# Filler matmuls on TensorE at the end of a cached-attention decode kernel

## The chip, the cores and the metric

The kernel runs on one core of a Trainium2 chip. The metric is the device time of one execution in microseconds (us), the median of several runs. Profiles are single executions; their span is about 1.9 us shorter than the device time of the same run.

## The reference

Two branches on one token are mixed by a sigmoid gate. Branch A is grouped-query attention with 32 query heads over a cache of 4 key/value heads and 65,536 positions; branch B is a small gated MLP.

```python
def reference(A_x, A_k_cache, A_v_cache, A_wq, A_wo, B_x, B_w_in, ..., gate_w):
    x = A_x                                     # 1 x 1 x 1024, bf16
    g = sigmoid((x * gate_w).sum(-1))
    q = (x @ A_wq)                              # 32 heads of 128
    p = softmax(q @ K^T * 128 ** -0.5)          # K cache: 4 x 65536 x 128, 64 MB
    a = (p @ V) @ A_wo                          # V cache as large; A_wo 4096 x 1024, 8 MB
    b = gelu_mlp(x, B_w_in, ..., B_w_out)
    return g * a + (1 - g) * b
```

All of K, V and the weights are read once, about 162 MB, for one output row of 1024 numbers. (The sizes of single tensors and tiles are in units of 2^20 bytes; the 162 MB is in units of 10^6.)

## The kernel before

One queue streams everything into five tiles of 4 MB that are reused; w_in comes in one piece of 7 MB, which is so in both kernels.

```python
    win = load(win_view, (KC, F), 3)
    win_t = [win[:, i * KH:(i + 1) * KH, :] for i in range(2)]
    ...
    def v_tile(g, j, vt):                # 32 matmuls of 512 columns, 64 output rows each
    ...
    def head_out(g):                     # last normalization of a head group, mostly VectorE
        nc.vector.tensor_tensor(out=om8, in0=o_ps[g]..., in1=own_8..., op=ALU.mult)
        nc.vector.tensor_reduce(out=o_sb[:], in_=om8.rearrange("p x d -> p d x"), ...)
        nc.tensor.matmul(om_ps[gs, DH:], lhsT=hs, rhs=lss[g][:], ...)
        nc.tensor.matmul(om_ps[gs, :DH], lhsT=hs, rhs=o_sb[:], ...)
        ...                              # five short VectorE steps that end in oa
    def project(w, n, vec, c0, first=False, last=False):
        for c in range(n):               # n rows of wo per partition
            for t in range(NB):          # 4 matmuls side by side, 32 output rows each
                nc.tensor.matmul(out_ps[t * B:(t + 1) * B, :],
                    lhsT=vec[:, c0 + c:c0 + c + 1].to_broadcast([P, B]),
                    rhs=w[:, c, t * NO:(t + 1) * NO], ...)
```

The end of the program, which the change touches (WO_SPLIT gives pieces of 16, 8, 4, 2, 1 and 1 rows):

```python
    for j, n, at in ((0, 2, 1), (2, 1, 3), (3, 1, 4)):
        for i, vt in enumerate(load_kv(A_v_cache, G - 1, j, at, n)):
            v_tile(G - 1, j + i, vt)
    head_out(G - 1)
    c0 = 0
    for at, split in enumerate(WO_SPLIT):
        for n in split:
            t = load(wo_view[:, c0:c0 + n, :], (n, D), ...)
            project(t, n, oa, c0, last=(c0 + n == OC))
            c0 += n
    nc.scalar.copy(out=out_sb[:], in_=out_ps[:])
    ...                                  # two stores of the row
```

Of the kernel before, what the change touches and what calls it, by code (L numbers as in the profile page):

```python
# [8 lines left out]
FP32 = mybir.dt.float32  # L9
# [6 lines left out]
P = 128  # L16
# [6 lines left out]
ZN = 448  # L23
HN = 512
WO_SPLIT = ((16,), (8, 4, 2, 1, 1))


@with_exitstack
def kernel(
# [15 lines left out]
    nc = tc.nc  # L45

    _, _, D = A_x.shape
    _, G, S, DH = A_k_cache.shape
# [15 lines left out]
    assert S % (P * CT) == 0 and F == 2 * NB * ZN and ZN == B * FC and HD == NHB * NB * HN  # L64
    assert NHB * NB == 2 * G and CC * B == 2 * HN and sum(map(sum, WO_SPLIT)) == OC

# [5 lines left out]
    pss = ctx.enter_context(tc.tile_pool(name="pss", bufs=2, space=bass.MemoryType.PSUM))  # L72
# [6 lines left out]
    def same_weights(ins):  # L79
        held.add(ins.ins.name)  # L80
# [79 lines left out]
    def load(src, shape, at):  # L160
        n = 1
        for s in shape:
            n *= s
        v = kv[:, int(at * CT * P):int(at * CT * P) + n]
        if len(shape) == 2:
            v = v.rearrange("p (a b) -> p a b", b=shape[1])
        ins = nc.sync.dma_start(out=v, in_=src)  # L167
        if not first_load:
            first_load.append(ins.ins.name)
        return v  # L170

    def load_kv(src, g, j, at, n=1):
        h, i = divmod(j, 2)
        rows = src[0, g, 2 * h * CT * P:2 * (h + 1) * CT * P, :].rearrange(
            "(p c) d -> p (c d)", c=2 * CT)
        v = load(rows[:, i * CT * DH:(i + n) * CT * DH], (n * CT * DH,), at)
        return [v[:, i * CT * DH:(i + 1) * CT * DH] for i in range(n)]
# [27 lines left out]
    wt = [big.tile([P, VC, BP, NB, VC, REP], BF16, name=f"wt{i}") for i in range(2)]  # L205
# [15 lines left out]
    def one_hot(shape, dtype, in0, col, name):  # L221
# [13 lines left out]
                     start=True, stop=True)  # L235
# [107 lines left out]
    for k in range(NHB):  # L343
# [15 lines left out]
                     rhs=q4[:].rearrange("p t x -> p (t x)"), start=True, stop=True)  # L359
# [71 lines left out]
    def v_tile(g, j, vt):  # L431
        if j == 0:
            o_ps[g] = pso.tile([P, 2, VC * DH], FP32, name="o_ps")
        vx = vt.rearrange("p (v c d) -> p c v d", v=VC, d=DH)
        for u in range(CC // 2):
            hs = slice(u % 2 * P // 2, (u % 2 + 1) * P // 2)
            for e in range(2):
                ins = nc.tensor.matmul(  # L438
                    o_ps[g][hs, e, :],
                    lhsT=ptt[g, j][:, 2 * u:2 * u + 2, :].rearrange("p c x -> p (c x)"),  # L440
                    rhs=vx[:, 2 * u + e], start=(j == 0 and u < 2),
                    stop=(j == NT - 1 and u >= CC // 2 - 2), skip_group_check=True)
                if e > 0:
                    same_weights(ins)

    def head_out(g):
        gs = slice(g * B, (g + 1) * B)
        nc.vector.tensor_tensor(  # L448
            out=om8, in0=o_ps[g][:].rearrange("p e (v d) -> p (e v) d", d=DH),
            in1=own_8[:].unsqueeze(2).to_broadcast([P, 2 * VC, DH]), op=ALU.mult)  # L450
        o_sb = wk.tile([P, DH], FP32, name="o_sb")
        nc.vector.tensor_reduce(out=o_sb[:], in_=om8.rearrange("p x d -> p d x"), axis=AX.X,  # L452
                                op=ALU.add)
        om_ps = psm.tile([P, DH + NT], FP32, name="om_ps", tag="m")
        hs = hsel[:].rearrange("p h q -> p (h q)")
        nc.tensor.matmul(om_ps[gs, DH:], lhsT=hs, rhs=lss[g][:], start=True, stop=True,
                         skip_group_check=True)
        nc.tensor.matmul(om_ps[gs, :DH], lhsT=hs, rhs=o_sb[:], start=True, stop=True,  # L458
                         skip_group_check=True)
        rl = wk.tile([P, 2], FP32, name="rl")  # L460
        nc.vector.reduce_sum(out=rl[gs, 0:1], in_=om_ps[gs, DH:], axis=AX.X)
        nc.vector.reciprocal(out=rl[gs, 1:2], in_=rl[gs, 0:1])
        om = wk.tile([P, QD, OC], FP32, name="om")
        nc.vector.tensor_tensor(
            out=om[gs], in0=om_ps[gs, :DH].rearrange("p (q c) -> p q c", c=OC),
            in1=own_q[gs, :].unsqueeze(2).to_broadcast([B, QD, OC]), op=ALU.mult)
        osum = wk.tile([P, OC], FP32, name="osum")
        nc.vector.tensor_reduce(out=osum[gs, :], in_=om[gs].rearrange("p q c -> p c q"),  # L468
                                axis=AX.X, op=ALU.add)
        nc.vector.tensor_scalar(out=oa[gs, :], in0=osum[gs, :], scalar1=rl[gs, 1:2],  # L470
                                scalar2=gate[gs, :], op0=ALU.mult, op1=ALU.mult)

    NO = D // NB
    out_ps = psl.tile([P, NO], FP32, name="out_ps")

    def project(w, n, vec, c0, first=False, last=False):
        for c in range(n):
            for t in range(NB):
                nc.tensor.matmul(  # L479
                    out_ps[t * B:(t + 1) * B, :],  # L480
                    lhsT=vec[:, c0 + c:c0 + c + 1].to_broadcast([P, B]),
                    rhs=w[:, c, t * NO:(t + 1) * NO],
                    start=(first and c == 0), stop=(last and c == n - 1),
                    skip_group_check=True)
# [22 lines left out]
    for j, n, at in ((0, 2, 1), (2, 1, 3), (3, 1, 4)):  # L507
        for i, vt in enumerate(load_kv(A_v_cache, G - 1, j, at, n)):
            v_tile(G - 1, j + i, vt)
    head_out(G - 1)  # L510


    wo_view = A_wo.rearrange("(p c) n -> p c n", c=OC)
    c0 = 0
    for at, split in enumerate(WO_SPLIT):
        for n in split:
            t = load(wo_view[:, c0:c0 + n, :], (n, D), at + c0 % (OC // 2) * D / (CT * P))
            project(t, n, oa, c0, last=(c0 + n == OC))
            c0 += n
    out_sb = const.tile([P, NO], BF16, name="out_sb")  # L520
    out_rows = out.rearrange("o t (q n) -> (o t q) n", n=NO)
    nc.scalar.copy(out=out_sb[:], in_=out_ps[:])  # L522
    for i, queue in enumerate((nc.scalar, nc.sync)):
        p0 = (2 * i + 1) * B - 1
        ins = queue.dma_start(out=out_rows[2 * i:2 * i + 2, :], in_=out_sb[p0:p0 + 2, :])
# [40 lines left out]
```

## Time and profile before

| | before |
|---|---|
| device time, first three runs | 383.21 us (383.08 to 383.30) |
| span of the profile | 381.3 us |
| bytes from HBM, mean rate | 162 MB, 425 GB/s |
| TensorE / VectorE busy | 60% / 57% |
| last piece of wo landed | 378.81 us |

The page of the profile cuts the span into 40 slices. Its rows give the granted TensorE clock and the busy share of the DMA engines in tenths.

```profile
span 381.3 us, 2579 instructions
...
PE 230.5 (60%) x1372; PEld 56.4 (15%) x796; DVE 218.4 (57%) x211; ACT 39.6 (10%) x55; POOL 4.4 (1%) x10
...
PEclk9995659998859995989589958895989579969766
DMA  9999999999999999999999999999999999999995
```

The DMA engines are at 9 tenths or more in every slice but the last: the kernel is bound by memory traffic. The Trainium skill, "DMA: Bandwidth & Descriptors", section "Where 436 GB/s comes from", puts the ceiling of the fabric at 435 GB/s; the mean here, 425 GB/s, lies just below it.

The chain of waits of before, its last pieces in order of time (start, length, what), without the pieces called issue, 0.04 us at most:

```profile
347.03 31.79 DMA kv<-in_A_wo_dram
378.86 0.43 PE out_ps L479 x4
379.31 0.37 ACT out_sb L522
```

The last wo load ends at 378.81 us. Only the four matmuls of the last row, ScalarE's copy and the store come after it. Of these, TensorE's clock can touch the 0.43 us alone.

The timeline of TensorE at the end of before (start, length, engine, line, operation, shape, count; in brackets the idle time before, and what ended it):

```profile
368.37 0.64 PE L458 MATMUL om_ps<-o_sb,hsel 128*32 128x128 f32 x2 [3.07 <-DVE o_sb L452]
370.39 4.64 PE L479 MATMUL out_ps<-kv,oa 128*32 128x256 bf16 x96 [1.39 <-DVE oa L470]
376.28 0.62 PE L479 MATMUL out_ps<-kv,oa 128*32 128x256 bf16 x16 [1.25 <-DMA kv<-in_A_wo_dram]
377.54 1.06 PE L479 MATMUL out_ps<-kv,oa 128*32 128x256 bf16 x12 [0.64 <-DMA kv<-in_A_wo_dram]
378.86 0.41 PE L479 MATMUL out_ps<-kv,oa 128*32 128x256 bf16 x4 [0.25 <-DMA kv<-in_A_wo_dram]
```

From 376.28 on, each group starts when its data land. TensorE is idle before each of them, so it is not late.

The same stretch of before, cut into windows of 3.41 us whose edges are those of the granted clock. The columns are the window, its length, then busy us (and records) of PE, PEld, DVE, ACT and POOL, then the granted clock, the DMA share and GB/s:

```profile
363.95:367.36 3.41, 1.35 (x14) 0.34 (x6) 2.14 (x2) 0.00 (x0) 0.00 (x0) 1.00 0.93 399
367.36:370.77 3.41, 1.02 (x10) 0.48 (x14) 2.14 (x6) 0.00 (x0) 0.00 (x0) 0.50 0.99 423
370.77:374.19 3.42, 3.42 (x72) 2.59 (x64) 0.00 (x0) 0.00 (x0) 0.00 (x0) 0.50 0.95 392
374.19:377.60 3.41, 1.52 (x52) 1.10 (x44) 0.00 (x0) 0.00 (x0) 0.00 (x0) 1.00 0.85 329
377.60:381.01 3.41, 1.35 (x16) 0.43 (x15) 0.00 (x0) 0.37 (x1) 0.00 (x0) 0.50 0.05 19
```

The clock is either full or half, and it changes only at these edges: a window that is busy enough is followed by one at full clock, a slack one by one at half. The last row, after 377.60, meets the half clock. Two windows of before from the middle of the kernel, each with its successor, bear on how much is enough for full-width matmuls of 512 columns: seven kept the clock, six lost it. (The DMA columns count a packet whole in the window in which it starts, so a short window can show more than 1.00 and more than the mean rate.)

```profile
200.11:203.52 3.41, 1.37 (x7) 0.29 (x3) 3.41 (x2) 0.00 (x0) 0.00 (x0) 1.00 0.93 404
203.52:206.94 3.42, 2.82 (x13) 0.57 (x6) 3.42 (x5) 0.00 (x0) 0.00 (x0) 1.00 1.20 517
237.65:241.07 3.42, 1.18 (x6) 0.28 (x3) 3.42 (x2) 0.00 (x0) 0.00 (x0) 1.00 1.20 517
241.07:244.48 3.41, 3.41 (x10) 0.60 (x5) 3.16 (x2) 0.00 (x0) 0.00 (x0) 0.50 0.89 384
```

In the profile of after:

```profile
200.26:203.67 3.41, 1.30 (x7) 0.29 (x3) 3.41 (x2) 0.00 (x0) 0.00 (x0) 1.00 0.85 365
203.67:207.09 3.42, 3.42 (x10) 0.58 (x4) 3.42 (x5) 0.00 (x0) 0.00 (x0) 0.50 1.20 517
```

### The profile page before, as it was taken

To read this page: it belongs to the slowest core of one execution; us is meant where nothing else is said; L and a number is where in the kernel's file an instruction comes from. 1 tells how busy PE (TensorE), PEld (TensorE's weight loads), DVE (VectorE), ACT (ScalarE), POOL (GpSimd) and SP (SyncE) were. 2 spreads that over 40 slices of the span, in tenths; PEclk is the share of its full clock that TensorE was granted. 3 is DMA by queue.
4 is the path that set the end of the run, shared out by engine and by line. 5 is a ranking of instruction groups with operands and counts; after the bars stand their busy time and mean duration, and the time that the engine had idled before them with its cause. 6 is when DMAs were issued, how large, how long until landed. Compare 5 with 4: busy or idle time off the path is not lost.

```text
span 381.3 us, 2579 instructions
## 1 busy us (share of the span) xinstructions
PE 230.5 (60%) x1372; PEld 56.4 (15%) x796; DVE 218.4 (57%) x211; ACT 39.6 (10%) x55; POOL 4.4 (1%) x10
## 2 busy tenths in 40 slices
PE   0064467678157934796397638872976196849355
PEld 0011011112011200121011101120111011212123
DVE  4133487996687506966977059669960488560040
ACT  1001001111601100114011001040100010500000
POOL 4000000000000000000000000000000000000000
PEclk9995659998859995989589958895989579969766
DMA  9999999999999999999999999999999999999995
GB/s 385 440 433 416 423 429 440 440 485 429 407 412 419 440 442 433 433 433 440 440 428 440 440 440 440 435 434 399 419 440 435 426 440 427 426 414 433 437 412 225
DMA packets 4231, 162.17 MB, mean 425 GB/s; under 512 B 504, under 2 KB 508, under 8 KB 892
## 3 DMA queue, kind: packets, MB, share of 16 engines
q1 hardware_dynamic: 4180, 162.01, 98.7%
q8 instruction: 8, 0.13, 0.1%
q14 instruction: 3, 0.02, 0.0%
q10 hardware_dynamic: 40, 0.01, 0.0%
HBM read 162.01 MB, written 0.00 MB: 425 GB/s over the span
## 4 chain that ended last, share of the span: by engine, by line
DMA 57%; PE 24%; DVE 14%; ACT 2%; issue 1%; SPq 1%; DVEq 0%; ACTq 0%
DMA kv<-in_A_k_cache_dram 42%; PE s_ps L392 20%; DMA kv<-in_A_wo_dram 8%; DVE kv L385 8%; DMA kv<-in_A_v_cache_dram 7%; PE o_ps L438 3%; DVE pt L428 2%; DVE o_sb L452 1%; DVE mx L387 1%; ACT sc L403 1%; ACT sc L425 1%; SPq L167 1%; DVE rowt L448 1%; PE om_ps L458 0%; DVE osum L468 0%
## 5 line engine op out<-in xcount | busy, mean ns | idle before, releaser
L392 PE MATMUL s_ps<-kv,wt 128*128 128x512 bf16 x512 | 140.3, 432 | 83.8 <-DVE kv L385 83.8
L385 DVE STREAM_TRANSPOSE kv<-kv 128x2048 int32<-128x2048 int32 x64 | 142.7, 2280 | 56.3 <-DMA kv<-in_A_k_cache_dram 56.3
L438 PE MATMUL o_ps<-kv,pt 128*64 128x512 bf16 x512 | 61.8, 400 | 7.5 <-DMA kv<-in_A_v_cache_dram 7.5
L392 PEld LDWEIGHTS <-wt 128*128 128x128 bf16 x256 | 27.3, 107 | 198.1 <-issue 138.0
L403 ACT CAST sc<-s_ps 128x1024 bf16<-128x1024 f32 x16 | 16.2, 1013 | 250.0 <-PE s_ps L392 250.0
L438 PEld LDWEIGHTS <-pt 128*64 128x64 bf16 x256 | 16.1, 115 | 50.6 <-issue 48.1
L428 DVE STREAM_TRANSPOSE pt<-sc 128x1024 bf16<-128x1024 bf16 x16 | 18.6, 1217 | 6.8 <-ACT sc L425 6.8
L387 DVE TENSOR_REDUCE mx<-sc 128x1 f32<-128x1024 bf16 x12 | 14.5, 1209 | 9.3 <-ACT sc L403 9.3
L425 ACT ACTIVATE sc<-sc,nb 128x1024 bf16<-128x1024 bf16 x16 | 18.2, 1136 | 12.2 <-DVE nb L421 12.2
L448 DVE TENSOR_TENSOR rowt<-o_ps,own 128x1024 f32<-128x1024 f32 x4 | 4.8, 1194 | 24.9 <-PE o_ps L438 24.9
L458 PE MATMUL om_ps<-o_sb,hsel 128*32 128x128 f32 x8 | 2.5, 422 | 19.7 <-DVE o_sb L452 19.7
L407 DVE TENSOR_REDUCE mx<-sc 128x1 f32<-128x1024 bf16 x4 | 4.9, 1220 | 14.4 <-ACT sc L403 14.4
L278 PE MATMUL q_ps<-kv,xT 128*32 128x512 bf16 x64 | 7.2, 630 | 3.7 <-DMA kv<-in_A_wq_dram 3.7
L479 PE MATMUL out_ps<-kv,oa 128*32 128x256 bf16 x128 | 6.7, 368 | 3.6 <-DMA kv<-in_A_wo_dram 2.1
L234 PE MATMUL xb_ps<-xg,spread 8*128 8x256 bf16 x1 | 0.4, 367 | 13.2 <-DMA xg<-in_gate_w_dram 13.2
L452 DVE TENSOR_REDUCE o_sb<-rowt 128x128 f32<-128x1024 f32 x4 | 7.5, 1872 | 0.1
L345 DVE TENSOR_TENSOR rowt<-q_ps,own_b 128x512 f32<-128x512 f32 x2 | 1.3, 685 | 8.8 <-PE q_ps L278 8.8
L278 PE MATMUL z_ps<-kv,xT 128*32 128x448 bf16 x64 | 6.0, 570 | 0.0
L479 PEld LDWEIGHTS <-oa 128*32 128x32 bf16 x128 | 4.4, 124 | 6.0 <-issue 3.2
L522 ACT CAST out_sb<-out_ps 128x256 bf16<-128x256 f32 x1 | 0.4, 372 | 45.3 <-PE out_ps L479 45.3
L238 DVE TENSOR_TENSOR xm<-xb_ps,sel_i 128x128 f32<-128x128 f32 x2 | 0.5, 286 | 8.0 <-PE xb_ps L234 8.0
L278 PEld LDWEIGHTS <-xT 128*32 128x32 bf16 x64 | 2.7, 141 | 11.9 <-issue 11.9
(88 smaller groups left out, 55.5 us busy)
## 6 DMA issues: line engine op xcount, KB each, us to landing
kv<-in_A_k_cache_dram SPq DMA_DIRECT2D x4, 4096.0 KB, 46.9
kv<-in_A_wq_dram SPq DMA_DIRECT2D x2, 4096.0 KB, 33.0
kv<-in_A_v_cache_dram SPq DMA_DIRECT2D x2, 4096.0 KB
kv<-in_B_w_in_dram SPq DMA_DIRECT2D x1, 7168.0 KB
kv<-in_A_wo_dram SPq DMA_DIRECT2D x1, 4096.0 KB
kv<-in_B_w_out_dram SPq DMA_DIRECT2D x1, 3584.0 KB
kv<-in_A_wo_dram SPq DMA_DIRECT2D x1, 2048.0 KB
kv<-in_A_wo_dram SPq DMA_DIRECT2D x1, 1024.0 KB, 30.6
```

What stands on the lines that cost most here:

```text
L278: ins = nc.tensor.matmul(ps[t * B:(t + 1) * B, k * HN:k * HN + n], lhsT=xT[:, i * KH + c:i * KH + c + 1].to_broadcast([P, B]), rhs=w[:, c, ...
L385: nc.vector.transpose(out=kb[:, v * n:(v + 1) * n], in_=kb[:, v * n:(v + 1) * n])
L387: nc.vector.reduce_max(**late.pop())
L392: ins = nc.tensor.matmul(s_ps[:, k * HN:(k + 1) * HN], lhsT=wt[g % 2][:, v, b].rearrange("p a v h -> p (a v h)"), rhs=kx[:, b // 2, b % 2, ...
L403: nc.scalar.copy(out=sct[g, j][:], in_=s_ps[:])
L407: nc.vector.reduce_max(**late.pop())
L425: nc.scalar.activation(out=sct[g, j][:], in_=sct[g, j][:], func=ACT.Exp, scale=SCALE, bias=nb[:, 0:1], accum_out=lss[g][:, j:j + 1])
L428: nc.vector.transpose(out=ptt[g, j][:].rearrange("p c x -> p (c x)"), in_=sct[g, j][:])
L438: ins = nc.tensor.matmul(o_ps[g][hs, e, :], lhsT=ptt[g, j][:, 2 * u:2 * u + 2, :].rearrange("p c x -> p (c x)"), rhs=vx[:, 2 * u + e], sta ...
L448: nc.vector.tensor_tensor(out=om8, in0=o_ps[g][:].rearrange("p e (v d) -> p (e v) d", d=DH), in1=own_8[:].unsqueeze(2).to_broadcast([P, 2 ...
L452: nc.vector.tensor_reduce(out=o_sb[:], in_=om8.rearrange("p x d -> p d x"), axis=AX.X, op=ALU.add)
L479: nc.tensor.matmul(out_ps[t * B:(t + 1) * B, :], lhsT=vec[:, c0 + c:c0 + c + 1].to_broadcast([P, B]), rhs=w[:, c, t * NO:(t + 1) * NO], st ...
```

## The change

The intent is to keep TensorE busy in its waits between the last V tile and the last two rows of wo, so that its clock does not fall and the remaining matmuls run at full rate. The fillers multiply a block of `wt`, the tile with the queries spread out for the score matmuls, that is mostly zeros (it also holds one head group's query values, at one place in sixteen), and write to a score buffer that nobody reads. There are 16 of them, with 6 weight loads. No load, wait or buffer of the real work changes. That w_in is loaded in one piece, as the change's description has it, is so in both kernels; it is not in the diff.

```diff
+WO_BUSY = {16: 4, 8: 2, 4: 1, 2: 1, 1: 0}
...
+    def keep_busy(n):
+        ps = pss.tile([P, 2 * HN], FP32, name="busy_ps", tag="s")
+        w = wt[G % 2][:].rearrange("p v b t u h -> p (v b t u h)")
+        for i in range(n):
+            ins = nc.tensor.matmul(ps[:, :HN], lhsT=w[:, :P], rhs=w[:, :HN], start=True,
+                                   stop=True, skip_group_check=True)
+            if i > 0:
+                same_weights(ins)
...
+    keep_busy(4)
     head_out(G - 1)
+    keep_busy(4)
...
             project(t, n, oa, c0, last=(c0 + n == OC))
+            keep_busy(WO_BUSY[n])
             c0 += n
```

## The prediction

> **What bounds the kernel.** HBM traffic. The page shows 162 MB at 425 GB/s over a span of 381.3 us, with the DMA row at 9 tenths in 39 of 40 slices; TensorE is busy 60%, VectorE 57%. The chain of waits ends: 31.79 us of wo DMA (to 378.81), 0.43 us for the last four output matmuls, 0.37 us of ScalarE copying the row, then the store, end at 381.3. Only what follows the last landing can be shortened by a faster TensorE.
>
> **The tail of before** (timeline):
> - 359.15: last V tile, 32 matmuls, 6.00 us, about 0.43 us each pair-half: cold clock until 364.0.
> - 365.2 to 370.3: head_out, mostly VectorE; TensorE idles 3.07 and 1.39 us.
> - 370.39: 24 rows of wo, 96 matmuls, 4.64 us, mostly cold.
> - 376.28 (4 rows), 377.54 (2+1 rows), 378.86 (last row): each begins when its DMA lands. Idle before them 1.25, 0.64, 0.25 us: TensorE already waits for DMA at every step.
>
> **The clock.** Busy time and granted clock in stretches of 3.41 us, cut so that an edge falls at 364.0, give almost pure values: 1.00 or 0.50. The clock falls at 367.4, rises at 374.2, falls at 377.6. So the last row runs cold. This agrees with the Trainium skill, "TensorE: Matmul & The Clock Gate", Part 1 (half rate after an idle window of about 3.4 us, full rate after a busy one). In this trace a stretch keeps the full clock with 7 full-width 512-column matmuls (200.15 to 203.56) and loses it with 6 (237.70 to 241.11). Four 32-column matmuls run side by side, so the stretch 374.2 to 377.6 with 48 matmuls of 256 columns counts as 6: lost.
>
> **What the change does.** w_in is loaded the same way in both; no DMA, wait or buffer changes. It adds 16 matmuls of 128x512 (4+4 around head_out, then 4, 2, 1, 1) plus 6 weight loads. Warm, about 0.22 us each (estimate: half of the 0.43 us cold spacing): 3.5 us of TensorE time, all in idle stretches. Counted as above, the stretch from 364.0 rises to about 10 matmuls, from 367.4 to 7 or 8, from 370.8 to about 12, from 374.2 to 7 or 8. Narrowly, the clock should stay full to the end. Matmuls of wo go from 417 ns to about 270 ns (the shortest record of that line).
>
> **On the critical path.** The 24 rows finish about 2 us sooner, but then wait for the landing at 376.2 as before. head_out is VectorE time and also hidden: wo lands until 378.8 anyway. Only the last four matmuls count: 0.43 becomes about 0.30 us. Expected gain 0.1 us of 383.2, below the spread of the runs (0.22). Should the clock stay cold, a filler (0.43 us) after the 2-row piece might delay the last row by up to 0.1 us. Landing of wo is unchanged.
>
> **Predicted:** 383.1 us, range 382.5 to 383.7. Faster by over 2%: 0.01; within 2%: 0.98; slower by over 2%: 0.01.
>
> **What would show it right.** Granted clock near 1.0 from 364 to the end (or falling only in some 3.41 us stretch); output matmuls near 270 ns; longer waits for wo DMA before the 4-row piece (over 1.25 us counted from the last projection); last landing still near 378.8; last four matmuls about 0.30 us; copy and store unchanged; busy TensorE total changed little, since fillers replace slow matmuls.
>
> **What would make it wrong.** The last landing moves, by something that I don't see linked to TensorE; the phase of the 3.41 us stretches against the kernel differs from run to run, so that the last row is already warm in some runs of before, or still cold after; or a filler waits for a score buffer (ScalarE's copies were done by about 330, so it should not).

## The result, and the profile after

| | before | after |
|---|---|---|
| device time | 383.10 us (383.08 to 383.30, 6 runs) | 383.12 us (382.94 to 383.16, 6 runs) |
| span of the profile | 381.3 us | 381.3 us |
| last piece of wo landed | 378.81 us | 378.86 us |
| four matmuls of the last row | 0.43 us | 0.32 us |

The ratio of the times is 0.9998, with a 95% interval from 0.9985 to 1.0011. Ratios here are the mean time of one kernel's runs over the mean of the other's of the same rounds, so they are not quite the ratio of the medians.

The page of after, the lines that answer to those of before:

```profile
span 381.3 us, 2601 instructions
...
PE 233.9 (61%) x1388; PEld 56.2 (15%) x802; DVE 218.5 (57%) x211; ACT 39.6 (10%) x55; POOL 4.4 (1%) x10
...
PEclk9995659899859895989688958895989579969799
...
```

The last two digits of the clock row are 9 9; before had 6 6. The DMA row, cut here, is the same as before.

The windows of after at the edges of its own clock, with columns as above:

```profile
364.10:367.51 3.41, 2.27 (x17) 0.37 (x5) 2.19 (x2) 0.00 (x0) 0.00 (x0) 1.00 0.96 413
367.51:370.93 3.42, 2.04 (x30) 0.88 (x31) 2.10 (x6) 0.00 (x0) 0.00 (x0) 1.00 0.96 407
370.93:374.34 3.41, 2.76 (x72) 1.67 (x61) 0.00 (x0) 0.00 (x0) 0.00 (x0) 1.00 0.97 401
374.34:377.75 3.41, 2.18 (x47) 1.07 (x38) 0.00 (x0) 0.00 (x0) 0.00 (x0) 1.00 0.83 321
377.75:381.17 3.42, 1.09 (x17) 0.32 (x9) 0.00 (x0) 0.37 (x1) 0.00 (x0) 1.00 0.03 9
```

The clock is full in all five windows. The timeline of TensorE in after shows what that does:

```profile
368.81 1.04 PE L478 MATMUL busy_ps<-wt 128*128 128x512 bf16 x4
370.27 1.93 PE L489 MATMUL out_ps<-kv,oa 128*32 128x256 bf16 x64 [0.42 <-DVE oa L471]
372.13 1.04 PE L478 MATMUL busy_ps<-wt 128*128 128x512 bf16 x4
373.81 1.06 PE L489 MATMUL out_ps<-kv,oa 128*32 128x256 bf16 x32 [0.65 <-DMA kv<-in_A_wo_dram]
374.80 0.60 PE L478 MATMUL busy_ps<-wt 128*128 128x512 bf16 x2
376.31 0.62 PE L489 MATMUL out_ps<-kv,oa 128*32 128x256 bf16 x16 [0.90 <-DMA kv<-in_A_wo_dram]
...
378.90 0.29 PE L489 MATMUL out_ps<-kv,oa 128*32 128x256 bf16 x4 [0.35 <-DMA kv<-in_A_wo_dram]
```

The first 16 rows of wo (64 matmuls) now end at 372.20 us; in before their last record ended at 374.0. But then the 8-row piece has not landed, and TensorE waits for it until 373.81. The 24 rows end at 374.87 instead of 375.03, 0.16 us sooner, and the 4-row piece starts at 376.31 instead of 376.28. What the fillers won was turned into waits for the wo loads. Nor can they change when a load starts: the queue has issued the last load of wo by 347.56 us, and the first filler starts at 365.18 us.

The chain of waits of after, cut in the same way:

```profile
347.12 31.74 DMA kv<-in_A_wo_dram
378.90 0.32 PE out_ps L489 x4
379.24 0.37 ACT out_sb L535
```

The last four matmuls took 0.11 us less, and in this execution the last load landed 0.05 us later. The first is 0.03% of the time; runs of one kernel differ by more.

### The profile page after: what moved, and what is told of

It reads as the page before. It is cut to its first block, busy times and chain, and to the rows that moved or that the text cites. A ratio compares the mean times of both kernels' runs of the same rounds, so it can differ in the third digit from the quotient of the medians. Undisturbed runs are those within 1.5% of the kernel's fastest.

```text
span 381.3 us, 2601 instructions
## 1 busy us (share of the span) xinstructions
PE 233.9 (61%) x1388; PEld 56.2 (15%) x802; DVE 218.5 (57%) x211; ACT 39.6 (10%) x55; POOL 4.4 (1%) x10
## 4 chain that ended last, share of the span: by engine, by line
DMA 58%; PE 25%; DVE 13%; ACT 2%; issue 1%; SPq 1%; DVEq 0%; ACTq 0%
DMA kv<-in_A_k_cache_dram 42%; PE s_ps L393 21%; DMA kv<-in_A_wo_dram 8%; DVE kv L386 7%; DMA kv<-in_A_v_cache_dram 7%; PE o_ps L439 3%; DVE pt L429 2%; DVE o_sb L453 1%; DVE mx L388 1%; ACT sc L404 1%; ACT sc L426 1%; SPq L168 1%; DVE rowt L449 1%; PE om_ps L459 0%; DVE osum L469 0%
## 5 line engine op out<-in xcount | busy, mean ns | idle before, releaser
L393 PE MATMUL s_ps<-kv,wt 128*128 128x512 bf16 x512 | 141.9, 438 | 81.9 <-DVE kv L386 81.9
L489 PE MATMUL out_ps<-kv,oa 128*32 128x256 bf16 x128 | 4.6, 274 | 2.7 <-DMA kv<-in_A_wo_dram 2.2
L478 PE MATMUL busy_ps<-wt 128*128 128x512 bf16 x16 | 4.5, 383 | 0.0
```

What stands on the lines that cost most here:

```text
L393: ins = nc.tensor.matmul(s_ps[:, k * HN:(k + 1) * HN], lhsT=wt[g % 2][:, v, b].rearrange("p a v h -> p (a v h)"), rhs=kx[:, b // 2, b % 2, ...
L489: nc.tensor.matmul(out_ps[t * B:(t + 1) * B, :], lhsT=vec[:, c0 + c:c0 + c + 1].to_broadcast([P, B]), rhs=w[:, c, t * NO:(t + 1) * NO], st ...
```

## The experiments

Each diff is against the changed kernel. The theory: only what follows the last landing counts, so the fillers can win the difference between four matmuls at half and at full clock, 0.11 us at most. Rivals: the fillers cost something (delayed matmuls, slower loads) that eats a larger gain; the sooner projection reaches the end; or the zeros are special. Before took 383.22 us beside late_only, early_only, real_data and win_two, 383.13 us beside big_last_none, big_last_fill, long_fill and one_less, and 383.31 us beside before_look1, before_look2, early_look and robust.

### Late fillers only (late_only)

```diff
-WO_BUSY = {16: 4, 8: 2, 4: 1, 2: 1, 1: 0}
+WO_BUSY = {16: 0, 8: 2, 4: 1, 2: 0, 1: 0}
-    keep_busy(4)
     head_out(G - 1)
-    keep_busy(4)
```

> Only three of the sixteen fillers stay: two after the 8-row piece of wo, one after the 4-row piece. Theory (only the clock of the four matmuls after the last landing counts): the stretch from 364 runs cold as in before, 24 rows of wo take about 4.6 us again, but the stretch 374.3 to 377.7 counts about 8 full-width matmuls instead of 5.5, so the clock stays 1.00 to the end and the last four matmuls take about 0.32 us as with all sixteen; time within 0.1 us of the changed kernel. Rival (the early fillers are what holds the clock, or the sooner projection matters): the clock falls at about 377.7 and the last four take 0.43 us.

Measured: 383.05 us, ratio to before 0.9995 (0.9983 to 1.0008). The window 367.68 to 374.51 ran at half clock, 96 matmuls took 4.72 us, the window 374.51 to 377.92 counted 8.5 full-width matmuls (columns times output rows of the matmuls that start in it, over 512 times 128), and the last four matmuls took 0.32 us. So the last row was at full clock with three fillers as with sixteen. This agrees with the theory, but one profile cannot show that the fillers did it: before itself ended at full clock in two of three profiles (below).

### Early fillers only (early_only, early_look)

```diff
-WO_BUSY = {16: 4, 8: 2, 4: 1, 2: 1, 1: 0}
+WO_BUSY = {16: 4, 8: 0, 4: 0, 2: 0, 1: 0}
```

> The twelve fillers around head_out and after the 16-row piece stay, the four later ones go. Theory: the clock is full from 364 to about 377.7, the stretch 374.3 to 377.7 counts about 4.5 full-width matmuls, fewer than 7, so the clock falls at about 377.7 and the last four matmuls take 0.43 us as in before, although the 24 rows finish 1 us or more sooner; time equal to before within 0.1 us. Rival (early speed-up of the projection reaches the end): the end comes sooner than in before by more than 0.1 us.

Measured: 383.10 us, ratio to before 0.9998 (0.9984 to 1.0011). The time met the expectation, the clock did not. The edges of the windows lay elsewhere in this execution, at 369.71, 373.13 and 376.54. The clock fell at 369.71 in spite of the fillers, rose at 373.13, and was full at the last row, which took 0.32 us. So the expectation had taken for granted that the edges stand still against the kernel, and they don't. The same kernel was run again:

> The kernel with the twelve early fillers alone, once more, because its first profile had an edge at 376.54 and none between it and the last row. Theory: if this time an edge lies between about 377.2 and 378.8, the stretch before it counts 5 or fewer and the last four matmuls take 0.43 us; if the last edge lies near 376.5 again, 0.32 us again. Rival (early fillers suffice): 0.32 us with any edge.

Measured: 383.13 us, ratio 0.9995 (0.9977 to 1.0013). The last edge before the last row lay at 376.13, so the case that would tell the theories apart did not come up; the row took 0.32 us. Inconclusive: whether early fillers suffice at every position of the edges stays open.

### The kernel before, profiled again (before_look1, before_look2)

The kernel is unchanged.

> The kernel before, unchanged, once more, because the profiles so far show the 3.41 us stretches of the clock at different places against the kernel (the last edge before the last landing lay between 376.4 and 378.4 us). Theory: which clock meets the last four matmuls in before depends on that place; they take 0.43 us where the stretch before them counted below 6 full-width matmuls and 0.32 us where it counted 6 or more, and the last landing stays at 378.9 within 0.2 us. Rival: before always ends cold, 0.43 us, wherever the edges lie.

Measured: 383.25 us, ratio 0.9998 (0.9980 to 1.0016). The last edge before the last row lay at 377.08, the window before it counted 6.0, the clock was kept, and the last landing was at 378.92, all within the theory; the rival failed.

> The kernel before, unchanged, a third profile: as for the first repeat. With an edge after about 377 the last four matmuls should take 0.43 us, with the last edge before about 376 they can take 0.32 us.

Measured: 383.21 us, ratio 0.9997 (0.9979 to 1.0015). In both, without a single filler, the last row met the full clock. The chain of waits of the first repeat:

```profile
378.96 0.32 PE out_ps L479 x4
```

And windows of the second repeat at its edges:

```profile
373.84:377.26 3.42, 1.64 (x49) 1.24 (x48) 0.00 (x0) 0.00 (x0) 0.00 (x0) 1.00 0.88 345
377.26:380.67 3.41, 0.99 (x16) 0.40 (x15) 0.00 (x0) 0.37 (x1) 0.00 (x0) 1.00 0.12 45
```

The edges lay only 0.34 us sooner than in the first profile of before, and the clock was kept. The expectation of the second repeat failed in its detail: an edge after 377 should have meant the half clock. By the same count this window holds 5.5, and so does the window 374.19 to 377.60 of the first profile, which lost the clock. Its busy time is larger, 1.64 us against 1.52 us. My count is too coarse for these narrow matmuls. What the three profiles do show is that before ended at half clock in one of them. The 0.11 us is not even there to be won in every run.

### The disputed cost made eight times larger (big_last_none, big_last_fill)

Wo comes in pieces of 16, 8 and 8 rows, so that 32 matmuls follow the last landing instead of 4. The fillers are now chosen by the first row of a piece: big_last_fill has 4 after the 16 rows and 14 after the first 8.

```diff
-WO_SPLIT = ((16,), (8, 4, 2, 1, 1))
-WO_BUSY = {16: 4, 8: 2, 4: 1, 2: 1, 1: 0}
+WO_SPLIT = ((16,), (8, 8))
+WO_BUSY = {0: 0, 16: 0, 24: 0}     # big_last_none; it also drops both keep_busy(4)
+WO_BUSY = {0: 4, 16: 14, 24: 0}    # big_last_fill
...
-            keep_busy(WO_BUSY[n])
+            keep_busy(WO_BUSY[c0])
```

> No fillers; wo comes in pieces of 16, 8 and 8 rows, so that 32 matmuls follow the last landing. This makes the disputed cost eight times larger. Theory: last landing still near 378.8, clock falls at about 377.7 (the stretch before counts about 3), the last 32 matmuls take about 2.07 us cold (31 times 53 ns and one of 417 ns); time about 1.6 us longer than before, 384.7 us.

Measured: 384.45 us (384.29 to 384.61), ratio to before 1.0035 (1.0022 to 1.0047). The clock fell at 377.13. The last landing was at 378.73, and the timeline of TensorE has:

```profile
378.77 1.90 PE L489 MATMUL out_ps<-kv,oa 128*32 128x256 bf16 x32 [3.83 <-DMA kv<-in_A_wo_dram]
```

I had expected 384.7 us and 2.07 us for these matmuls, a little too much of both.

> The same pieces of 16, 8 and 8 rows with fillers: 4 and 4 around head_out, 4 after the 16 rows, 14 after the first 8. Theory: clock 1.00 to the end, the last 32 matmuls take about 1.06 us, so about 1.0 us (0.26%) less than the same pieces without fillers, about 383.7 us, still longer than before; the last landing at the same time within 0.1 us. Rival (fillers cost what they gain, for instance because their reads slow the landing): equal times, or a later landing.

Measured: 383.90 us (383.61 to 383.92), ratio to before 1.0018 (1.0005 to 1.0030). The clock was full to the end:

```profile
375.01 3.19 PE L478 MATMUL busy_ps<-wt 128*128 128x512 bf16 x14
378.92 1.06 PE L489 MATMUL out_ps<-kv,oa 128*32 128x256 bf16 x32 [0.71 <-DMA kv<-in_A_wo_dram]
```

Every run with fillers is below every run without. From the two ratios, 1.0018 / 1.0035 is 0.9983, about 0.65 us of 384; the profiles have 1.90 against 1.06 us, 0.84 us. I had expected 1.0. So fillers do gain time where matmuls follow the last landing, and the more the more of them follow: in the profiles the matmuls took 0.11 us less for 4 and 0.84 us less for 32. The landing was 0.14 us later with fillers (378.87 against 378.73), a little over the 0.1 us that I allowed; 0.84 less 0.14 is 0.70 us, by which the two profiles' spans differ (382.8 and 382.1 us). In eleven profiles with the original pieces and without the long run of fillers it lies anywhere from 378.69 (robust, which has the most fillers of them) to 378.98 (real_data), and in the three of before from 378.81 to 378.92, so nothing shows that fillers slow the loads, though with one profile each a delay of 0.1 us is not excluded either. Both kernels stay slower than before, which keeps its last piece small.

### Fillers that outlast the last landing (long_fill)

```diff
-WO_BUSY = {16: 4, 8: 2, 4: 1, 2: 1, 1: 0}
+WO_BUSY = {16: 4, 8: 2, 4: 1, 2: 16, 1: 0}
```

> The changed kernel with 16 fillers instead of 1 after the 2-row piece, so that they outlast the last landing. Theory: they run from 377.9 to about 381.4, the last two rows follow at once, and the end comes about 2.5 us later than in the changed kernel (385.6 us): TensorE's order makes a filler critical as soon as it passes the last landing, and not before. Rival (fillers can be overtaken or cost little): less than 1 us later.

Measured: 385.84 us, ratio to before 1.0073 (1.0057 to 1.0088). The timeline of TensorE:

```profile
377.77 3.63 PE L478 MATMUL busy_ps<-wt 128*128 128x512 bf16 x15
381.33 0.40 PE L489 MATMUL out_ps<-kv,oa 128*32 128x256 bf16 x8
```

The last two rows wait for the fillers, and the time grows by 2.7 us over before. The last load landed at 378.71 us, as in the other runs, and the last rows start at 381.33 us. So fillers cost nothing that shows until they cross the last landing, and from then on the time that is left of them.

### One filler fewer (one_less) and other data (real_data)

```diff
 # one_less
-WO_BUSY = {16: 4, 8: 2, 4: 1, 2: 1, 1: 0}
+WO_BUSY = {16: 4, 8: 1, 4: 1, 2: 1, 1: 0}
 # real_data
-        w = wt[G % 2][:].rearrange("p v b t u h -> p (v b t u h)")
+        w = kv[:, 4 * CT * P:4 * CT * P + HN]
```

> The changed kernel with one filler instead of two after the 8-row piece. The stretch 374.3 to 377.7 then counts 6.5 full-width matmuls; before has kept the clock with 7.0 and lost it with 6.0, so this tells on which side the limit lies; either way the time changes by at most 0.15 us. If the clock stays, the last four matmuls take 0.32 us, if it falls, 0.43 us.

Measured: 383.16 us, ratio 1.0001 (0.9983 to 1.0019). The last edge lay at 376.45, the window before it counted 9, and the last four took 0.32 us. So the limit was not met where I wanted to test it, and this run says nothing of it there.

> The fillers multiply the last V tile's numbers instead of the mostly zero block. Theory (the clock follows how much TensorE streams, not the values): granted clock 1.00 from 364 to the end, last four matmuls 0.32 us, same time within 0.2 us. Rival (zeros are special, or reading the V tile disturbs): clock pattern or landing differ by more than that.

Measured: 383.21 us, ratio 1.0000 (0.9982 to 1.0018). The last four took 0.32 us and the landing was at 378.98. But the clock was at half from 369.60 to 373.01, which the theory had not expected. The pair of runs explains it. The windows of real_data and then of one_less:

```profile
366.19:369.60 3.41, 1.38 (x6) 0.23 (x3) 2.81 (x6) 0.00 (x0) 0.00 (x0) 1.00 0.94 399
369.60:373.01 3.41, 3.34 (x64) 2.43 (x64) 0.01 (x1) 0.00 (x0) 0.00 (x0) 0.50 0.98 416
```

```profile
366.21:369.62 3.41, 1.40 (x10) 0.25 (x10) 2.73 (x6) 0.00 (x0) 0.00 (x0) 1.00 0.99 423
369.62:373.03 3.41, 3.41 (x64) 2.40 (x64) 0.00 (x0) 0.00 (x0) 0.00 (x0) 0.50 0.96 404
```

Their edges lie within 0.02 us of each other, and the mostly zero block loses the clock in the same window as the V tile's numbers. In this pair it is the position of the edges that decides, and not the data. Only four of the fillers start in these windows; the four before head_out fall before the edge. With edges there, even the eight fillers around head_out don't hold the clock.

### w_in in two pieces (win_two)

```diff
-    win = load(win_view, (KC, F), 3)
-    win_t = [win[:, i * KH:(i + 1) * KH, :] for i in range(2)]
+    win_t = [load(win_view[:, i * KH:(i + 1) * KH, :], (KH, F), 3 + i * KH * F / (CT * P))
+             for i in range(2)]
```

> The changed kernel with w_in loaded in two pieces of half the rows instead of one. Theory (HBM bound, the first projection hidden behind the loads): the first matmuls on w_in start about 8 us sooner, the last wo landing stays at 378.9 within 0.3 us, time within 0.3 us of the changed kernel. Rival (the single piece matters to the start): the last landing moves by more than 0.5 us.

Measured: 383.16 us, ratio to before 0.9998 (0.9984 to 1.0012). The first matmuls on w_in start at 12.63 us instead of 20.49 us, and the last load lands at 378.77. One piece or two is hidden behind the loads.

### More late fillers (robust)

```diff
-WO_BUSY = {16: 4, 8: 2, 4: 1, 2: 1, 1: 0}
+WO_BUSY = {16: 4, 8: 4, 4: 3, 2: 1, 1: 0}
```

> The changed kernel with 4 fillers instead of 2 after the 8-row piece and 3 instead of 1 after the 4-row piece, so that a stretch ending anywhere between 375.5 and 378.8 counts at least 7. Theory: full clock at the last row wherever the edges lie, last four matmuls 0.32 us, no delay of the last row; and the time still cannot be told from before (at most 0.1 us, 0.03%, less). Rival: the fillers push the last row (over 0.05 us between last landing and first of the last four).

Measured: 383.20 us (382.96 to 383.25), ratio to before 0.9997 (0.9983 to 1.0011). The window 374.00 to 377.41 counted 10.4, the clock was full, and the last four took 0.32 us, 0.04 us after the landing. One profile cannot show that it holds at every position of the edges. It can't be told from before or from the changed kernel by its time, so no version here beats both.

## Why the prediction was right, and where its steps were off

- The total was right: 383.1 us predicted, 383.12 us measured, and no change that could be told from noise. The reason given, that only the last four matmuls follow the last landing, is what the runs show: made eight times longer, that part gained 0.65 us by fillers; made to wait for fillers, it cost 2.7 us.
- The size of that part was right where before ends at half clock: about 0.30 us predicted and 0.32 us measured, from 0.43 us. The gain itself, 0.1 us, is too small for these times to show; it is read from the profiles alone.
- "The 24 rows finish about 2 us sooner" was wrong. They finished 0.16 us sooner. The first 16 rows ended 1.8 us sooner, and then TensorE waited for the landing of the 8-row piece, which before had hidden behind slow matmuls. It did not matter for the total, because the wait for the 4-row piece came behind it.
- The count that was to decide the clock was wrong as a rule. In other profiles full-width windows of seven lost the clock and windows of five and six kept it. For the narrow matmuls it gave six for the window of before from 374.2; by starts it is 5.5, since a record that crosses an edge is listed on both sides. And 5.5 kept the clock in one profile and lost it in another.
- "The clock should stay full to the end" held in the profile of after. In four other profiles with the same fillers around head_out (early_only, early_look, one_less and real_data) it fell at an edge between 369.31 (early_look) and 369.72 us (early_only). So that it held in the profile of after was luck of where the edges lay. The Trainium skill, "TensorE: Matmul & The Clock Gate", Part 1, "What's actually happening", says that the window is free-running and does not restart with the kernel; the runs agree, with the last edge before the last row anywhere from 376.13 (early_look) to 378.08 us (win_two), not counting long_fill with its late last row.
- The warning that "the last row is already warm in some runs of before" came true in two of three profiles of before. The expected gain of 0.1 us is thus what a run can gain that would have ended at half clock, not a mean over runs.
- Added cost was as predicted: fillers of about 0.22 us each, all in waits for data or VectorE. Four of them took 1.04 us from first start to last end, the last one's own record being 0.38 us, so (1.04 - 0.38) / 3 = 0.22 us apart.

Open: how often before ends at half clock; the exact rule by which matmuls, narrow ones above all, count for the clock; and whether the early fillers alone would suffice at every position of the edges.

## What to carry to other kernels

Ask what stands between the last landing of a load and the end of the program, because in a kernel bound by loads like this one, once all loads are issued, only that part answers to a faster engine; everything sooner became a longer wait here. Fillers that hold TensorE's clock are free while they fit into such waits, and gain more the more matmuls follow the last landing, so a small last piece leaves them almost nothing to gain. One profile shows one position of the clock's windows: profile an unchanged kernel several times before a half-clock stretch at one place is called its cost.

## What the Trainium skill lacked or had wrong

- "TensorE: Matmul & The Clock Gate", Part 1, names an idle window as what takes the clock away, and gives no measure of how busy a window must be. Here windows of full-width matmuls at full clock kept it with 1.36 us or more of busy TensorE and lost it with 1.34 us or less, but for one of 1.40 us; at half clock they were followed by full clock with 2.67 us or more and not with 2.60 us or less. Windows of narrow matmuls, four side by side, kept it with 1.64 us and lost it with 1.52 us.
- "DMA: Bandwidth & Descriptors", "Where 436 GB/s comes from", says that for loads from HBM the HBM side of about 358 GB/s binds. With one core running, 162 MB came from HBM at a mean of 425 GB/s. A note of the same page has its measurements, 425 GB/s at most, as single-core ones, with which this agrees; so it is that sentence that needs the condition.
- No page was found that sizes how far the sixteen DMA engines drift apart on one long queue. In before the last piece's sixteen completions lie between 376.67 and 378.81 us, and the DMA share is 0.61 from 376.28 to 377.54 and 0.17 from there to 378.81. This idle share at the end is far more than the 0.11 us at stake here; no run tried to win it.
